# Two decode layers on one core: in the second pass, GpSimd multiplies three of eight key tiles by the query for the first two units

## The chip, the cores and the metric

The kernel runs on one core of a Trainium2 chip. The metric is the device time of one execution in microseconds. TensorE is called PE in the profile, its weight loads PEld, VectorE DVE, ScalarE ACT, GpSimd POOL, and SyncE, which issues nearly all DMAs here, SP.

## The reference

Two rounds of the same two blocks, each with a layer norm ahead and a residual sum behind, for batch 2, one query token, 16 heads of width 256 and 4096 cached keys, all in float32:

```python
q = (x @ wq).reshape(B, Sq, H, Dh).transpose(0, 2, 1, 3)
scores = einsum("bhqd,bhkd->bhqk", q, k_cache) * Dh ** -0.5
o = einsum("bhqk,bhkd->bhqd", softmax(scores), v_cache)
x = x + (o in one row per batch) @ wo
gate, up = x_n @ W_gate, x_n @ W_up
x = x + (relu(gate) * up) @ W_down
```

Attention, feed-forward, attention, feed-forward: both attentions read the whole cache, 32 key rows and 32 value rows of 4 MB each.

## The kernel before

**Units.** One unit `u` is one (head, batch) pair, so an attention pass has 32 units. Its 4096 keys lie as 128 partitions by 32 tiles of 256 numbers. They are handled in four chunks (`c` = 0 to 3) of eight tiles, 1 MB each; values likewise. `order[u]` says which pair a unit is; the second pass begins with the pairs that the first ended with, and most of the keys and values of its first units are still in SBUF.

**Scores.** With one query row a matrix product would leave PE mostly empty, so scores are elementwise products and sums. `score(u, c)` has two ways for a tile. Either DVE does product and sum in one instruction (`scalar_tensor_tensor`, L547), or DVE multiplies several tiles at once (`tensor_mul`, L534) and ACT sums each of these tiles (L540). In the first five units of the second pass (`HASTE`) a chunk is split four and four, except in the first two chunks of unit 0, where DVE does all eight. The query `q_of[u]` of units 0 and 1 lies in PSUM (`po[0]`, `po[1]`); that of unit 2 on is spread to all partitions in SBUF by POOL (`partition_broadcast`, L447).

**Softmax.** `softmax_max(u)`: DVE takes each partition's maximum (L556), POOL the maximum over partitions (`partition_all_reduce`, L558). `softmax_exp(u)`: ACT scales it (L563), takes exponentials and their sum (L567), and POOL adds the sums (L574). `weigh(u, c)` then multiplies a chunk of values by the exponentials on PE (L602).

**What sets the order.** Each engine runs its instructions in the order in which the program wrote them, and waits where it must. SP works off one list of loads in a fixed order (`pump`, L156). A load goes out when the SBUF slot that it is to fill has been released, which `release` does after the last use of what lay there; the loads behind it on the list wait too. Around the change the list reads: the four key chunks of unit 3, into the slots of unit 0's key chunks; the four key chunks of unit 4, into the slots of unit 1's key chunk 0, unit 0's value chunk 0, unit 1's key chunk 1 and unit 0's value chunk 1; two pieces of 2 MB with unit 3's values, after unit 1's key chunk 3 and unit 0's value chunk 3; two pieces of 2 MB with unit 5's keys, after unit 2's key chunk 1 and unit 1's value chunk 1; two of 2 MB with unit 4's values, after unit 2's key chunk 3 and unit 1's value chunk 3; 0.9 MB of weights; then loads of 4 MB and more.

**Start of the second pass.** `first_query` takes the query of unit 0 from the feed-forward block's end, computes the deviation for the layer norm (`Sqrt`, L386) and has ACT do one unread `Exp` (L464), before which ACT loads its table.

Of the kernel before, what the change touches and what calls it, by code (L numbers as in the profile page):

```python
# [14 lines left out]
B, D, H, S, DH, F = 2, 448, 16, 4096, 256, 1792  # L15
P = 128
# [3 lines left out]
CT = 8  # L20
UNIT = CT * DH
NC = NT // CT
# [10 lines left out]

GROUPED = 14
MIDDLE = BLOCKS * PAIR + 1
SUMS = 96
SPACED = 2 * NT + 2
HASTE = 5
# [5 lines left out]
SCALE = DH**-0.5  # L44
# [35 lines left out]
def two_layers(  # L80
# [10 lines left out]
    nc = tc.nc  # L91
# [44 lines left out]
    def pump():  # L136
        while pending:
            (kind, name, c), n = pending[0]
            last = at_of.get((kind, name, c - 1)) if kind in "kv" else None
            if kind == "g":  # L140
                last = MIDDLE - (name + 1) % 2
            at = units.take(n, kind, last)
# [26 lines left out]
    def place(at):  # L169
        packed = max(0, at - BLOCKS * PAIR)  # L170
        return at * UNIT - packed * (UNIT - F)

    def get(*key):
        if key in lies_at:
            return arena[:, lies_at[key] : lies_at[key] + F]
        at = at_of[key]
        return arena[:, place(at) : place(at + 1)]
# [105 lines left out]
    row = consts.tile([P, D], F32, name="row")  # L283
    down = consts.tile([P, D], F32, name="down")
    junk = down[:, :DH]
    spaced = [down[:, DH + i * SPACED : DH + (i + 1) * SPACED] for i in range(2)]
    y_end_row = extra[SUMS : SUMS + B, :TAIL]
    nc.scalar.dma_start(row[:B, :D], x.rearrange("b s d -> (b s) d"))
# [36 lines left out]
    rstd = little("rstd", B, bufs=1)  # L325

    po = [ps_o.tile([P, 2 * DH], F32, name=f"po{i}") for i in range(2)]
# [6 lines left out]
    nc.vector.memset(acc, 0.0)  # L334
    y = acc[SUMS : SUMS + B]

# [46 lines left out]
    def deviation(total):  # L383
        var = ps_s.tile([P, B], F32, name="small")
        nc.tensor.matmul(var, ones.to_broadcast([P, P]), total, start=True, stop=True)
        nc.scalar.activation(rstd, var, AF.Sqrt, bias=eps_t, scale=1.0 / D)  # L386

    def inverse():
        nc.vector.reciprocal(rstd, rstd)

    def attention(order, after, q_first=None, begun=None):
# [3 lines left out]
        nsr = little("nsr", B, bufs=1)  # L395
        sr = little("sr", B, bufs=1)
        aside = []
        q_of, oT_of, s_of, mx_of, p_of, r_of, po_of, pT_of = ({} for _ in range(8))
        n_u = len(order)


        def query_of(u, pq):
            h, b = order[u]
            parts = query_parts(h)
            for c, cols, w in parts:
                nc.tensor.matmul(
                    pq[:, b, cols], xT[:, c, b : b + 1].to_broadcast([P, P]), w,
                    start=(c == 0), stop=(c == parts[-1][0]),
                )
            q_of[u] = pq[:, b, :]  # L410
# [41 lines left out]
        def first_query():  # L452


            if q_first is None:
                total = squares()
                query_of(0, po[0].rearrange("p (b n) -> p b n", b=B))
            else:
                q_of[0] = q_first
                total = begun()  # L460
            deviation(total)
            query_of(1, po[1].rearrange("p (b n) -> p b n", b=B))
            unread = little("sums", 1)
            nc.scalar.activation(unread, eps_t, AF.Exp)  # L464

        def score_block(u, c):

# [39 lines left out]
        def score(u, c):  # L507
            kept = ("k", order[u], c) in after
            if ("k", order[u]) in blocks and not kept and not (ahead and u < HASTE):
                return score_block(u, c)  # L510
            kt = get("k", order[u], c).rearrange("p (t n) -> p t n", t=CT)
            if c == 0:
                s_of[u] = little("scores", NT)
            found = s_of[u][:, c * CT : (c + 1) * CT]
            by_act = 0 if kept else BY_ACT
            part = kt
            if kept and aside:
                by_act = CT // 2 - c % 2
                at = c % 2 * (CT // 2) * DH
                part = aside[0][:, at : at + by_act * DH].rearrange("p (t n) -> p t n", t=by_act)  # L520
            whole = CT
            if ahead and (u < HASTE or u >= n_u - CLOSING):
                by_act = CT // 2 if u > 0 or c > 1 else 0
                last = u == n_u - 1 and c == NC - 1
                whole = by_act if u < HASTE or last else CT
                if whole == CT:
                    by_act = CT // 2 + 1
            whole = whole if by_act else 0
            if kept:
                whole = by_act  # L530
            if by_act:


                nc.vector.tensor_mul(  # L534
                    part[:, :whole, :],
                    kt[:, :whole, :],
                    q_of[u][:, None, :].to_broadcast([P, whole, DH]),
                )
                for t in range(by_act):
                    nc.scalar.activation(  # L540
                        part[:, t, :], part[:, t, :], AF.Copy, accum_out=found[:, t : t + 1]
                    )
            if whole > by_act:
                nc.vector.reduce_sum(found[:, by_act:], kt[:, by_act:, :], axis=AX.X)  # L544
            else:
                for t in range(whole, CT):
                    nc.vector.scalar_tensor_tensor(  # L547
                        junk if kept else kt[:, t, :], kt[:, t, :], 1.0, q_of[u],
                        op0=ALU.mult, op1=ALU.mult, accum_out=found[:, t : t + 1],
                    )  # L550
            if not kept:
                release("k", order[u], c)
# [93 lines left out]
        def project(u):  # L646
# [16 lines left out]
            elif ("h", h, 0) not in after:  # L663
                release("h", h, 0)

        def if_pair(step, u, *more):
            if 0 <= u < n_u:
                step(u, *more)

        first_query()  # L670
        nc.gpsimd.memset(down[:, DH : DH + 2 * SPACED], 0.0)

        ahead = 2 if ("k", order[0], 0) in keep else 0
        for u in range(n_u + 2):

            mixed = ahead and u < HASTE
            if_pair(score, u, 0)
            if_pair(out_add, u - 2)
            if_pair(out_turn, u - 2)
            asked = u % 2 and ahead < u + 1 < n_u  # L680
            if asked and ("h", order[u + 1][0], 0) in after:
                query(u + 1)
                asked = False
            if mixed:
                if_pair(weigh, u - 1, 0)
            if_pair(score, u, 1)
            closing = ahead and u == n_u - 1
            if closing:
                out_keep(u - 2)
                project(u - 2)  # L690
            if mixed:
                if_pair(weigh, u - 1, 1)
            if_pair(score, u, 2)
            if u == 0:
                inverse()
                nc.vector.tensor_scalar_mul(sr, rstd, SCALE)
                nc.vector.tensor_scalar_mul(nsr, rstd, -SCALE)
            if not closing:
                if_pair(out_keep, u - 2)
                if_pair(project, u - 2)  # L700
            if asked:
                query(u + 1)
            if u == n_u - 3 and after:
                slot = units.take(1, "h")
                aside.append(arena[:, place(slot) : place(slot + 1)])
            if ahead and u == 0:
                query(ahead)
            if_pair(softmax_sum, u - 1)
            if mixed:
                if_pair(weigh, u - 1, 2)  # L710
            if_pair(score, u, 3)
            if u % 2 and u < n_u and order[u][0] < GROUPED and order[u][0] % 2:
                release("q", order[u][0] // 2, 0)
            if u == n_u - 1 and aside:
                units.free.add(slot)
                pump()
            if_pair(softmax_max, u)
            if_pair(softmax_exp, u)
            for c in range(NC):
                if not mixed or c == NC - 1:  # L720
                    if_pair(weigh, u - 1, c)
            if_pair(out_copy, u - 1)

    def ffn(last):


        absorb(acc[:SUMS], SUMS, lead, nlead)
        busy(2)
# [53 lines left out]
        pg = proj(banks[0], [(0, 0, True), (1, 1, True), (2, 2, True), (3, 3, False)])  # L782
        add_rows(SUMS, lead, stop=last)
        if last:
            y_left = y[:, : FULL * P]
            left = down[SUMS : SUMS + B, : FULL * P]
            nc.vector.tensor_copy(left, y_left)
# [15 lines left out]
        if last:  # L803
            unit = ident[SUMS : SUMS + B, SUMS : SUMS + B]
            nc.tensor.matmul(y_left, unit, left, start=True, stop=False)
# [211 lines left out]
```

## Time and profile before

| | |
|---|---|
| median of 3 runs | 1314.49 us (1314.07 to 1314.73) |
| the profiled execution | 1314.92 us, of which the span is 1312.7 us |
| busy in the span | DVE 1067.1 us, PE 504.6, POOL 291.8, ACT 193.9 |
| moved by DMA | 561.26 MB, mean 428 GB/s |

The first pass fills the span up to about 650 us, the feed-forward block the stretch to 688 us, and the second pass starts with DVE's first product at 688.45 us. The page's "idle before" of an engine is time in which it waited; "issue" means that the profile shows nothing that it waited for.

### The profile page before, as it was taken

To read this page: it belongs to the slowest core of one execution; us is meant where nothing else is said; L and a number is where in the kernel's file an instruction comes from. 1 tells how busy PE (TensorE), PEld (TensorE's weight loads), DVE (VectorE), ACT (ScalarE), POOL (GpSimd) and SP (SyncE) were. 2 spreads that over 40 slices of the span, in tenths; PEclk is the share of its full clock that TensorE was granted. 3 is DMA by queue.
4 is the path that set the end of the run, shared out by engine and by line. 5 is a ranking of instruction groups with operands and counts; after the bars stand their busy time and mean duration, and the time that the engine had idled before them with its cause. 6 is when DMAs were issued, how large, how long until landed. Compare 5 with 4: busy or idle time off the path is not lost.

```text
span 1312.7 us, 8369 instructions
## 1 busy us (share of the span) xinstructions
PE 504.6 (38%) x3016; PEld 150.8 (11%) x3016; DVE 1067.1 (81%) x709; ACT 193.9 (15%) x784; POOL 291.8 (22%) x168
## 2 busy tenths in 40 slices
PE   3152253332433224424494535322343323433348
PEld 2010011000101001102141101000111000110013
DVE  4988989799897998787619897798999889886892
ACT  1100000010000000122416523000000000012231
POOL 0330412304123050021001253140345004100230
PEclk9566776656776667667697777666776666766669
DMA  9999999999999999999999999999999999999998
GB/s 408 435 434 430 436 432 431 437 424 432 444 419 440 439 430 421 441 423 428 422 400 417 433 425 440 435 439 428 425 439 432 435 429 436 433 434 421 431 421 342
DMA packets 19924, 561.26 MB, mean 428 GB/s; under 512 B 2216, under 2 KB 2348, under 8 KB 6572
## 3 DMA queue, kind: packets, MB, share of 16 engines
q1 hardware_dynamic: 19876, 560.74, 99.5%
q8 instruction: 23, 0.38, 0.1%
q14 instruction: 17, 0.14, 0.0%
q10 hardware_dynamic: 8, 0.00, 0.0%
HBM read 560.73 MB, written 0.00 MB: 427 GB/s over the span
## 4 chain that ended last, share of the span: by engine, by line
DMA 56%; DVE 29%; POOL 7%; PE 4%; issue 2%; ACT 1%; SPq 0%; POOLq 0%; DVEq 0%
DMA arena<-in_vk_dram 50%; DVE tiny L502 15%; DVE arena L488 10%; POOL tiny L574 5%; DMA arena<-in_w_in_dram 3%; DMA arena<-in_w_head_dram 3%; POOL tiny L558 2%; DVE arena L534 2%; DVE arena L547 1%; DMA arena<-in_w_out_dram 1%; PE po L602 1%; PE small L631 1%; ACT arena L540 1%; DVE tiny L544 0%; DVE row L620 0%
## 5 line engine op out<-in xcount | busy, mean ns | idle before, releaser
L488 DVE TENSOR_TENSOR arena<-arena 128x8192 f32<-128x8192 f32 (+2 forms) x53 | 450.9, 8509 | 106.3 <-DMA arena<-in_vk_dram 104.7
L502 DVE TENSOR_REDUCE tiny<-arena 128x32 f32<-128x8192 f32 (+2 forms) x54 | 437.0, 8093 | 0.0
L602 PE MATMUL po<-arena,down 128*4 128x512 f32 x2052 | 314.2, 732 | 186.8 <-ACT down L567 115.5
L558 POOL PARTITION_ALL_REDUCE tiny<-tiny x64 | 95.4, 1490 | 717.1 <-DVE tiny L556 716.3
L631 PE MATMUL small<-tiny,row 128*128 128x2 f32 x128 | 31.2, 348 | 571.9 <-DVE row L620 571.9
L574 POOL PARTITION_ALL_REDUCE tiny<-tiny x64 | 173.8, 2715 | 61.3 <-ACT down L567 61.3
L563 ACT ACTIVATE tiny<-tiny 128x1 f32<-128x1 f32 x64 | 18.8, 294 | 727.8 <-POOL tiny L558 727.8
L602 PEld LDWEIGHTS po<-arena,down 128*4 128x4 f32 x2052 | 65.1, 98 | 406.8 <-issue 226.8
L631 PEld LDWEIGHTS small<-tiny,row 128*128 128x128 f32 x128 | 28.5, 310 | 602.6 <-DVE row L620 602.6
L435 PE MATMUL pq<-arena,xs 128*33 128x512 f32 (+2 forms) x158 | 70.2, 600 | 0.0
L540 ACT ACTIVATE arena<-arena 128x256 f32<-128x256 f32 x134 | 53.9, 403 | 40.8 <-DVE arena L534 40.7
L654 PE MATMUL acc<-arena,tiny 128*2 128x448 f32 x128 | 50.2, 880 | 21.0 <-DVE tiny L644 21.0
L447 POOL PARTITION_BROADCAST arena<-arena x32 | 21.7, 748 | 162.2 <-ACT arena L443 162.2
L494 ACT ACTIVATE arena<-arena 128x256 f32<-128x256 f32 x112 | 44.8, 402 | 79.7 <-DVE arena L488 79.7
L534 DVE TENSOR_TENSOR arena<-arena 128x1024 f32<-128x1024 f32 (+2 forms) x21 | 32.7, 1558 | 4.7 <-PE acc L654 4.7
L443 ACT ACTIVATE arena<-pq 33x512 f32<-33x512 f32 (+1 forms) x16 | 8.8, 548 | 177.2 <-PE pq L435 177.2
L620 DVE SCALAR_TENSOR_TENSOR row<-po,tiny,row 128x256 f32<-128x256 f32 x32 | 15.3, 479 | 22.3 <-ACT row L616 22.3
L644 DVE TENSOR_TENSOR tiny<-small,tiny 128x4 f32<-128x4 f32 x32 | 5.1, 161 | 28.7 <-PE small L631 28.7
L567 ACT ACTIVATE down<-tiny 128x32 f32<-128x32 f32 x64 | 26.6, 416 | 2.2
L435 PEld LDWEIGHTS pq<-arena,xs 128*33 128x33 f32 x158 | 19.2, 131 | 64.4 <-issue 60.0
L540 ACT ACTIVATION_READ_ACCUMULATOR arena<-arena 128x1 f32 x134 | 25.0, 187 | 0.0
L494 ACT ACTIVATION_READ_ACCUMULATOR arena<-arena 128x1 f32 x112 | 20.9, 187 | 0.0
(151 smaller groups left out, 316.8 us busy)
## 6 DMA issues: line engine op xcount, KB each, us to landing
arena<-in_vk_dram SPq DMA_DIRECT2D x17, 4096.0 KB, 41.0
arena<-in_vk_dram SPq DMA_DIRECT2D x16, 2048.0 KB, 34.6
arena<-in_w_pair_dram SPq DMA_DIRECT2D x11, 1792.0 KB, 30.8
arena<-in_vk_dram SPq DMA_DIRECT2D x12, 1024.0 KB, 9.0
arena<-in_w_in_dram SPq DMA_DIRECT2D x12, 896.0 KB, 25.6
arena<-in_vk_dram SPq DMA_DIRECT2D x1, 6784.0 KB
arena<-in_w_head_dram SPq DMA_DIRECT2D x7, 896.0 KB, 31.2
arena<-in_w_out_dram SPq DMA_DIRECT2D x5, 896.0 KB, 19.6
```

Of the source, the lines that this page charges most:

```text
L435: nc.tensor.matmul(q[:, cols], xs[:, c, :], w_c, start=(i == 0), stop=(i == len(parts) - 1))
L488: nc.vector.tensor_mul(part, part, q_of[u][:, None, :].to_broadcast([P, n, DH]))
L494: nc.scalar.activation(kt[:, t, :], kt[:, t, :], AF.Copy, accum_out=s_of[u][:, t : t + 1])
L502: nc.vector.reduce_sum(found, part, axis=AX.X)
L534: nc.vector.tensor_mul(part[:, :whole, :], kt[:, :whole, :], q_of[u][:, None, :].to_broadcast([P, whole, DH]),)
L540: nc.scalar.activation(part[:, t, :], part[:, t, :], AF.Copy, accum_out=found[:, t : t + 1])
L558: nc.gpsimd.partition_all_reduce(mx_of[u], mx, P, RED.max)
L567: nc.scalar.activation(found, s_of.pop(u).rearrange("p (k r) -> p k r", r=2), AF.Exp, bias=nm, scale=sr[:, b : b + 1], accum_out=rs,)
L574: nc.gpsimd.partition_all_reduce(total[:, b : b + 1], rs, P, RED.add)
L602: nc.tensor.matmul(po_of[u][32 * t : 32 * t + 4, (i - 2 * t) * DH : (j - 2 * t) * DH], p_of[u][:, at : at + 4], values[:, i * DH : j * DH] ...
L631: nc.tensor.matmul(pT_of[u][:, c, :], row[:, c * P : (c + 1) * P], pick[:, b : b + B], start=True, stop=True,)
L654: nc.tensor.matmul(acc[at : at + B], oT_of[h][:, c, :], wo[:, c * D : (c + 1) * D], start=(n < 3), stop=(n >= n_u - 3),)
```

## The change

For units 0 and 1 of the second pass, three tiles of each chunk (`POOLED`) are multiplied by the query on POOL, in place in the key slot, and ACT sums these three as before; DVE does the other five in single instructions. Chunk 0 of unit 0 stays with DVE whole. The query is copied for POOL from PSUM into SBUF by DVE, into `row` for unit 0 and `down` for unit 1. POOL's products for chunks 1 to 3 of unit 0 are written at the pass's start, for chunk 0 of unit 1 before DVE's last chunk of unit 0, and for chunks 1 to 3 of unit 1 within that unit. The `Sqrt`, the unread `Exp` with the table load, the memset of `down` and the scales of the exponent come behind `softmax_max(0)`, and the query of unit 2 behind `softmax_exp(0)`. The first pass keeps its order.

```diff
+POOLED = 3
...
         def first_query():
             if q_first is None:
                 total = squares()
                 query_of(0, po[0].rearrange("p (b n) -> p b n", b=B))
+                spread_of(total)
             else:
                 q_of[0] = q_first
                 total = begun()
+                share(0, row[:, :DH], range(1, NC))
+            query_of(1, po[1].rearrange("p (b n) -> p b n", b=B))
+            return total
+
+        def spread_of(total):
             deviation(total)
-            query_of(1, po[1].rearrange("p (b n) -> p b n", b=B))
             unread = little("sums", 1)
             nc.scalar.activation(unread, eps_t, AF.Exp)
+
+        def share(u, room, chunks):
+            if u not in near:
+                nc.vector.tensor_copy(room, q_of[u])
+                near[u] = room
+            for c in chunks:
+                kt = get("k", order[u], c).rearrange("p (t n) -> p t n", t=CT)[:, :POOLED, :]
+                nc.gpsimd.tensor_mul(kt, kt, room[:, None, :].to_broadcast([P, POOLED, DH]))
...
-                by_act = CT // 2 if u > 0 or c > 1 else 0
+                by_act = CT // 2
+                if u < 2:
+                    by_act = POOLED if u + c > 0 else 0
+                    if u == 1 and c < NC - 1:
+                        share(1, near[1], [c + 1])
...
+                if u not in near:
+                    nc.vector.tensor_mul(part[:, :whole, :], ...)
...
             if_pair(score, u, 2)
-            if u == 0:
-                inverse()
-                nc.vector.tensor_scalar_mul(sr, rstd, SCALE)
-                nc.vector.tensor_scalar_mul(nsr, rstd, -SCALE)
+            if u == 0 and ahead:
+                share(1, down[:, :DH], range(1))
...
-            if ahead and u == 0:
-                query(ahead)
...
             if_pair(softmax_max, u)
+            if u == 0 and ahead:
+                nc.gpsimd.memset(down[:, DH : DH + 2 * SPACED], 0.0)
+                spread_of(total)
+                scales()
             if_pair(softmax_exp, u)
+            if ahead and u == 0:
+                query(ahead)
```

POOL at the program's start, the same before and after (line numbers of before). `ident` is the identity matrix that `make_identity` builds; a row "ISA" that names nothing is the one whose instruction the trace calls MODIFY_POOL_CONFIG; "ISA" rows with names are the all-reduces and broadcasts.

```order
masks.py:197 MEMSET ident 128x128
masks.py:199 ISA
masks.py:199 AFFINE_SELECT ident<-ident 128x128
L671 MEMSET down 128x132
L558 ISA
L558 ISA tiny<-tiny 128x1
L574 ISA tiny<-tiny 128x1
L447 ISA arena<-arena 128x256 x2
```

Such a row stands between a tensor instruction such as AFFINE_SELECT and the all-reduces, in either direction; these are the only two in the kernel before. At the start of the second pass, POOL before, from the last unit of the first pass to unit 1:

```order
L558 ISA tiny<-tiny 128x1
L574 ISA tiny<-tiny 128x1
L671 MEMSET down 128x132
L447 ISA arena<-arena 128x256 x2
L558 ISA tiny<-tiny 128x1
L574 ISA tiny<-tiny 128x1
```

The same place after (L481 the products of `share`, L580 and L596 the all-reduces for maximum and sum, L449 the broadcast, L744 the memset):

```order
L481 ISA
L481 TENSOR_TENSOR arena<-arena,row 128x768 x3
L481 TENSOR_TENSOR arena<-arena,down 128x768
L580 ISA
L580 ISA tiny<-tiny 128x1
L744 MEMSET down 128x132
L596 ISA tiny<-tiny 128x1
L449 ISA arena<-arena 128x256 x2
L481 ISA
L481 TENSOR_TENSOR arena<-arena,down 128x768 x3
L580 ISA
L580 ISA tiny<-tiny 128x1
```

Seven products are new, and four of the nameless rows: ahead of unit 0's products, between the fourth product and unit 0's maximum, between the broadcast and unit 1's last three products, and between these and unit 1's maximum.

DVE at the start of the second pass before, units 0 and the first half of unit 1:

```order
L547 SCALAR_TENSOR_TENSOR arena,tiny<-arena,po_101 128x256 x16
L534 TENSOR_TENSOR arena<-arena,po_101 128x1024
L547 SCALAR_TENSOR_TENSOR arena,tiny<-arena,po_101 128x256 x4
L389 RECIPROCAL tiny<-tiny 128x2
L696 TENSOR_SCALAR tiny<-tiny 128x2
L697 TENSOR_SCALAR tiny<-tiny 128x2
L534 TENSOR_TENSOR arena<-arena,po_101 128x1024
L547 SCALAR_TENSOR_TENSOR arena,tiny<-arena,po_101 128x256 x4
L556 TENSOR_REDUCE tiny<-tiny 128x1
L534 TENSOR_TENSOR arena<-arena,po_102 128x1024
L547 SCALAR_TENSOR_TENSOR arena,tiny<-arena,po_102 128x256 x4
```

After, all of units 0 and 1:

```order
L477 COPY row<-po_101 128x256
L569 SCALAR_TENSOR_TENSOR arena,tiny<-arena,po_101 128x256 x18
L477 COPY down<-po_102 128x256
L569 SCALAR_TENSOR_TENSOR arena,tiny<-arena,po_101 128x256 x5
L578 TENSOR_REDUCE tiny<-tiny 128x1
L390 RECIPROCAL tiny<-tiny 128x2
L690 TENSOR_SCALAR tiny<-tiny 128x2
L691 TENSOR_SCALAR tiny<-tiny 128x2
L569 SCALAR_TENSOR_TENSOR arena,tiny<-arena,po_102 128x256 x20
L578 TENSOR_REDUCE tiny<-tiny 128x1
```

The six products of four tiles are gone from DVE, 40 single-tile instructions have become 43, and two copies are added. Unit 1's maximum (the last row) still stands ahead of everything that DVE does for unit 2.

More of the change, by code (lines that the diff above doesn't have):

```diff
@@ L397, in attention @@
         aside = []
+        near = {}
         q_of, oT_of, s_of, mx_of, p_of, r_of, po_of, pT_of = ({} for _ in range(8))
@@ L531, in score @@
             if by_act:
[L534 to L538, printed above, removed]
+                if u not in near:
+                    nc.vector.tensor_mul(
+                        part[:, :whole, :],
+                        kt[:, :whole, :],
+                        q_of[u][:, None, :].to_broadcast([P, whole, DH]),
+                    )
                 for t in range(by_act):
@@ L664, in project, with scales @@
                 release("h", h, 0)
+        def scales():
+            inverse()
+            nc.vector.tensor_scalar_mul(sr, rstd, SCALE)
+            nc.vector.tensor_scalar_mul(nsr, rstd, -SCALE)
         def if_pair(step, u, *more):
@@ L668, in if_pair @@
                 step(u, *more)
-        first_query()
-        nc.gpsimd.memset(down[:, DH : DH + 2 * SPACED], 0.0)
+        total = first_query()
         ahead = 2 if ("k", order[0], 0) in keep else 0
@@ L693, in attention @@
             if_pair(score, u, 2)
-            if u == 0:
-                inverse()
-                nc.vector.tensor_scalar_mul(sr, rstd, SCALE)
-                nc.vector.tensor_scalar_mul(nsr, rstd, -SCALE)
+            if u == 0 and ahead:
+                share(1, down[:, :DH], range(1))
+            if u == 0 and not ahead:
+                nc.gpsimd.memset(down[:, DH : DH + 2 * SPACED], 0.0)
+                scales()
             if not closing:
@@ L717, in attention @@
             if_pair(softmax_max, u)
+            if u == 0 and ahead:
+                nc.gpsimd.memset(down[:, DH : DH + 2 * SPACED], 0.0)
+                spread_of(total)
+                scales()
             if_pair(softmax_exp, u)
+            if ahead and u == 0:
+                query(ahead)
             for c in range(NC):
```

## The prediction

> **What bounds the kernel now.** I read the profile's page first, for what is never idle.
>
> ```profile
> DMA  9999999999999999999999999999999999999998
> q1 hardware_dynamic: 19876, 560.74, 99.5%
> HBM read 560.73 MB, written 0.00 MB: 427 GB/s over the span
> ```
>
> SP's one queue keeps the 16 DMA engines busy for 99.5% of the span. So the kernel is bound by its loads: 1 MB (1.049 million bytes) takes 2.46 us at 427 GB/s, and engine time counts only where a slot comes free so late that the queue runs dry. Next I asked the windows view about the stretch that the change touches (the last number of a row is GB/s).
>
> ```profile
> 690.00:698.00 8.00, 4.08 (x22) 2.91 (x22) 7.97 (x38) 4.80 (x18) 0.70 (x2) 0.97 1.02 422
> 698.00:706.00 8.00, 4.54 (x32) 0.88 (x32) 7.59 (x29) 5.81 (x27) 0.98 (x3) 0.60 1.01 384
> 706.00:714.00 8.00, 1.75 (x16) 0.26 (x12) 7.59 (x29) 5.50 (x26) 1.70 (x2) 0.83 1.00 422
> ```
>
> Here the queue does run nearly dry: 384 GB/s for 8 us instead of 422, so 8 x 38/422 = 0.7 us of transfer is lost. SP's own waits from 690 to 712 us say on whom: on DVE's single-tile scores. SP's loads say how full the queue is: time from issue to landing for the loads issued at 699.7 us (1 MB, after unit 0's key chunk 3), 705.3 (1 MB, after unit 1's chunk 1), 715.9 (2 MB, after unit 2's chunk 1) and 730.4 (0.9 MB), and for one of 0.9 MB at 669.3, in the pause at the feed-forward block.
>
> ```profile
> SPq L156 <- DVE arena L547: 22.5, 8, 4.4
> ...
> L156 SPq DMA_DIRECT2D arena<-in_vk_dram x1: 328/328/328, 699.7 to 699.7; - x1
> DMA to landing us min/median/max: 6.2/6.2/6.2
> ...
> L156 SPq DMA_DIRECT2D arena<-in_vk_dram x1: 328/328/328, 705.3 to 705.3; - x1
> DMA to landing us min/median/max: 9.3/9.3/9.3
> ...
> L156 SPq DMA_DIRECT2D arena<-in_vk_dram x1: 327/327/327, 715.9 to 715.9; - x1
> DMA to landing us min/median/max: 15.8/15.8/15.8
> ...
> L156 SPq DMA_DIRECT2D arena<-in_w_pair_dram x1: 328/328/328, 730.4 to 730.4; - x1
> DMA to landing us min/median/max: 18.2/18.2/18.2
> ...
> L156 SPq DMA_DIRECT2D arena<-in_w_in_dram x1: 328/328/328, 669.3 to 669.3; - x1
> DMA to landing us min/median/max: 5.6/5.6/5.6
> ```
>
> An empty queue thus lands 1 MB about 6.2 us after its issue, so 2 MB after about 8.6 (2.46 more). At 699.7 the queue is empty; afterwards it fills: by 730.4 the wait ahead of a load is 18.2 - 5.6 = 12.6 us. So at this one place a release that comes earlier gains at most 0.7 us, and one that comes later is paid in full once the small store is used up.
>
> **What the change takes from DVE.** The prices are these.
>
> ```profile
> 688.45 0.42 DVE L547 SCALAR_TENSOR_TENSOR arena<-arena,po 128x256 f32<-128x256 f32 x1 [0.66 <-PE po L892]
> 693.92 1.22 DVE L534 TENSOR_TENSOR arena<-arena,po 128x1024 f32<-128x1024 f32 x1
> 679.70 0.56 DVE L819 COPY row<-po 128x384 f32<-128x384 f32 x1 [0.64 <-PE po L813]
> L534 DVE TENSOR_TENSOR arena<-arena,pq 128x768 f32<-128x768 f32 x4 | 3.8, 942 | 0.0
> ```
>
> Sixteen single-tile instructions lie between 688.45 and 693.92: 0.342 us each. Six products of 1.22 go (7.3 us), three singles (1.0) and two copies come; a copy of 256 columns, two thirds of the 0.56 row, is 0.4. Net 4.5 us less for DVE. New DVE times: copy to 688.85; chunk 0 released at 691.6 (the first two releases of before fall due at 688.45 + 8 x 0.342 = 691.2 and 693.9); chunk 1 after five singles at 693.3, chunk 2 at 695.0, copy to 695.4, chunk 3 at 697.1.
>
> **POOL's products.** POOL's rows from the program's start and ahead of the second pass:
>
> ```profile
> 0.73 0.20 POOL masks.py:197 MEMSET ident<- 128x128 f32 x1 [0.29 <-POOLq L1012]
> 12.15 0.28 POOL masks.py:199 TENSOR_SCALAR_AFFINE_SELECT ident<-ident 128x128 f32<-128x128 f32 x1 [11.21 <-issue]
> 39.13 0.38 POOL L558 PARTITION_ALL_REDUCE tiny<-tiny  x1 [26.53 <-DVE tiny L556]
> ...
> 689.50 0.21 POOL L671 MEMSET down<- 128x132 f32 x1 [38.55 <-PE acc L374]
> ```
>
> No row shows a product on POOL. Below, DVE's 0.94 us for the same 128x768; above, I scale POOL's only arithmetic on a tile, 0.28 us for 128x128, by six: 1.7 us. I take 1.7, since it is POOL's own row. Unit 0's three run from 688.9 to 694.0, ahead of DVE's chunk 3, and the first of unit 1 from 695.4, after the second copy, to 697.1. So unit 0 goes well: its last release comes 2.6 us before that at 699.7.
>
> **The nameless rows on POOL.** The order shows four of them in the new stretch. Before has two, both at the program's start, and the trace calls them so:
>
> ```profile
> masks.py:199 POOLq MODIFY_POOL_CONFIG  x2: 11/11/11, 1.0 to 1.0; - x2
> ...
> L558 POOLq MODIFY_POOL_CONFIG  x2: 1/1/1, 12.8 to 12.8; - x2
> ```
>
> MODIFY_POOL_CONFIG itself takes nothing, but the AFFINE_SELECT behind it starts 11.2 us after the memset, its only input, was done, and nothing else is named for that wait. I read it as a switch of POOL's code, of about X = 11.2 us. The second, at 12.8 us, ends somewhere inside 26.3 us of waiting for DVE, so it bounds X only from above; but it shows that a switch hides behind a wait, since the all-reduce then starts at once with its usual 0.38 us. So of the four the first is free: POOL idles for 38.6 us up to 689.5. The other three stand between work that is ready.
>
> The Trainium skill, in GPSIMD Engine Reference, section Instruction dispatch, gives about 6 us, measured 5.95, for the code load behind a MODIFY_POOL_CONFIG. Here the row has nearly twice that. By the Trainium skill the sum below would come to 2 x 5.95 - 5.5 = 6.4 us.
>
> **The chain behind the switches.** Its links from before:
>
> ```profile
> 697.30 0.95 POOL L447 PARTITION_BROADCAST arena<-arena  x2 [7.59 <-ACT arena L443]
> 700.10 0.35 POOL L558 PARTITION_ALL_REDUCE tiny<-tiny  x1 [1.85 <-DVE tiny L556]
> 701.41 0.38 POOL L574 PARTITION_ALL_REDUCE tiny<-tiny  x1 [0.96 <-ACT down L567]
> ...
> 696.78 0.36 ACT L443 ACTIVATE arena<-pq 33x256 f32<-33x256 f32 x1
> ...
> 700.81 0.42 ACT L567 ACTIVATE down<-tiny 128x32 f32<-128x32 f32 x1
> ...
> L540 ACT ACTIVATE arena<-arena 128x256 f32<-128x256 f32 x24 | 9.7, 403 | 5.0 <-DVE arena L534 5.0
> ...
> 721.03 0.19 DVE L556 TENSOR_REDUCE tiny<-tiny 128x1 f32<-128x32 f32 x1 [0.39 <-ACT arena L540]
> ```
>
> - Switch 2: 697.1 to 708.4. Unit 0's maximum, ready on DVE at 697.3, waits for it; before, it started at 700.10. From its start to ACT's end of the exponential are 1.1 us, and 0.1 for handing over: 709.6. PE's `weigh(0)`, and with it value slots, waits for that.
> - ACT then copies the query of unit 2 (0.36) and sums unit 1's chunk 0 (3 x 0.40): released at 711.2. The broadcast ends by 0.52 + 0.95 from the copy's start, at 711.1.
> - Switch 3: 711.1 to 722.3. Products of unit 1's chunks 1 to 3: 724.0, 725.7, 727.4. ACT's three sums: 1.25 us with the handing over, so chunk 1 is released at 725.3 and chunk 3 at 728.7.
> - DVE's maximum of unit 1 stands ahead of its unit 2 and waits for the last of these sums; DVE, done with unit 1's 20 singles at about 697.7 + 6.8 = 704.5, idles for 24 us.
> - Switch 4: 727.4 to 738.6, then unit 1's maximum and exponential. ACT reaches unit 2's sums only at 739.8; eight of them end at 743.0, sixteen at 746.2. Before, DVE took unit 2's maximum at 721.03, so engines run 25 us late.
>
> **The sum, in landings.** After unit 1's chunk 1: issued 725.3, landed 731.5 on an empty queue; before, 705.3 + 9.3 = 714.6. That is 2X - 5.5 = 16.9 us late. The 2 MB after unit 2's chunk 1: issued 743.0, landed 751.6; before, 715.9 + 15.8 = 731.7. That is 3X - 13.7, or 19.9 us late, and the larger of the two counts. Behind it the pieces go out faster than they move, and where engines are 25 us late against the queue's 20, the 12.6 us of store at 730.4 cover the other 5. The lost 0.7 us is inside these landings. What is lost to the queue is lost at the end: 20 us, 1314.9 to 1334.9 us for the profiled execution, 1314.5 to 1334.5 us for the median, which lies 0.4 below it.
>
> The table load costs nothing: ACT's `Sqrt`, load and `Exp` lie beside switch 2, and if that were free they would still end by about 697.2, before the maximum is back. The 4.5 us saved on DVE end in its wait.
>
> **Rivals.**
>
> - *A shorter switch.* Nearly half of the 11.2 us belong to the program's start, where more may be cold, and X is 6. Against it: no row has it shorter. The first landing decides, 2 x 6 - 5.5 = 6.5 us: 1321 us. The figure of the Trainium skill above is this case.
> - *Two kinds of switch.* The 11.2 us were towards tensor instructions, as switch 3; 2 and 4 go to the all-reduces, for which I have only the 26.3 us above. With 6 for those, the first landing gives 6 + 11.2 - 5.5 = 11.7 us: 1326 us.
> - *No switch to pay.* The code stays resident after the first time, or the 11.2 us were the start of the program. Then unit 1's chunks are released at 700.3 to 706.5, chunk 1 at 703.1 (before 705.3), the queue never dries, and the 0.7 us come back: 1313.8 us, not slower. It decides from X below 5.5/2 = 2.75 us. For it: the trace has no packets that I could call code. Against it: the order writes out all four.
> - *A longer switch* under a full DMA queue: 13 us would give 3 x 13 - 13.7 = 25 us, 1340 us.
>
> **How the numbers follow.** X of 11.2 for all three: 0.45, so 1334.5 us. Two kinds: 0.19. Shorter: 0.2. No switch: 0.1. Longer: 0.06. The range takes in all but no switch and the longest: 1319 us (X of 5, 4.5 us) to 1340. A measurement of this kernel can tell about 0.2%, 2.6 us, from no change. Faster by that much needs more than the 0.7 us there are: 0.02. Within it: no switch, or X up to 4: 0.09. Slower: 0.89.
>
> **What would show it.** In the changed kernel's trace: POOL idle for about 11 us by "issue" ahead of unit 0's maximum, of unit 1's second product and of unit 1's maximum; products of about 1.7 us; DVE idle some 24 us ahead of unit 1's maximum, released by ACT; two windows between 705 and 745 us far below 420 GB/s, about 20 us of transfer in sum. Gaps of 6 us give 1321; none, with unit 1's maximum near 705 us, would make the forecast wrong.

## The result, and the profile after

The changed kernel takes 1331.5 us (median of 4 runs, 1330.9 to 1334.5) against 1314.5 us (1314.1 to 1314.7): 1.0134 times, 95% interval 1.0117 to 1.0152, or 17.0 us more. The forecast was 1334.5 us in a range of 1319 to 1340. The profiled execution is the slowest of the four, 1334.5 us; two more traces below show where 3 us of it come from.

From the page of the changed kernel: the loads are the same, and they take longer.

```profile
q1 hardware_dynamic: 19876, 560.74, 98.2%
HBM read 560.73 MB, written 0.00 MB: 421 GB/s over the span
```

The windows view of the changed kernel shows where (last number: GB/s).

```profile
690.00:698.00 8.00, 4.07 (x23) 2.95 (x22) 7.90 (x48) 7.11 (x31) 6.76 (x4) 0.93 1.02 398
698.00:706.00 8.00, 0.00 (x0) 0.00 (x0) 7.30 (x44) 0.07 (x1) 0.12 (x1) 0.50 0.90 371
706.00:714.00 8.00, 2.74 (x16) 0.56 (x20) 0.00 (x0) 2.26 (x10) 1.89 (x5) 0.51 0.08 14
714.00:722.00 8.00, 2.17 (x21) 0.29 (x12) 0.00 (x0) 0.00 (x0) 0.00 (x0) 0.92 0.63 250
722.00:730.00 8.00, 0.00 (x0) 0.00 (x0) 0.83 (x2) 3.92 (x18) 5.32 (x3) 0.50 0.42 148
730.00:738.00 8.00, 0.00 (x0) 0.00 (x0) 6.91 (x27) 0.00 (x0) 0.00 (x0) 0.50 1.03 429
738.00:746.00 8.00, 5.85 (x32) 0.95 (x32) 2.67 (x10) 6.76 (x34) 0.77 (x2) 0.59 0.73 276
```

Against 420 GB/s the windows from 698 us on lose 8 x (49 + 406 + 170 + 272 + 144)/420 = 19.8 us of transfer (the one at 730 loses none); the kernel before lost 0.7 us there. Within a us that is the whole difference of the two profiled executions, 1334.5 - 1314.9 = 19.6 us. From 714 to 722 us DVE, ACT and POOL show no work at all: these three wait for something that shows as no instruction.

POOL's timeline says for whom (start, duration, line; in brackets the idle time before and what ended it; L481 are the products, L580 and L596 the all-reduces for maximum and sum, L449 the broadcast).

```profile
689.72 5.35 POOL L481 TENSOR_TENSOR arena<-arena,row 128x768 f32<-128x768 f32 x3 [38.35 <-DVE row L477]
696.31 1.80 POOL L481 TENSOR_TENSOR arena<-arena,down 128x768 f32<-128x768 f32 x1 [1.24 <-issue]
709.90 0.38 POOL L580 PARTITION_ALL_REDUCE tiny<-tiny  x1 [11.79 <-issue]
...
711.80 0.97 POOL L449 PARTITION_BROADCAST arena<-arena  x2
722.48 5.32 POOL L481 TENSOR_TENSOR arena<-arena,down 128x768 f32<-128x768 f32 x3 [9.71 <-issue]
738.79 0.38 POOL L580 PARTITION_ALL_REDUCE tiny<-tiny  x1 [10.99 <-issue]
```

Three pauses of 11.8, 9.7 and 11.0 us stand between a product and an all-reduce or broadcast, or the other way round, and nothing but "issue" ends them. The first change of kind, ahead of 689.72, is covered by the 38.35 us of waiting for DVE.

Who waits behind them: ACT's scaling of the maximum, which stands ahead of the exponentials (L585), ACT's sums (L562), and DVE's maximum of unit 1 (L578).

```profile
710.31 0.29 ACT L585 ACTIVATE tiny<-tiny 128x1 f32<-128x1 f32 x1 [12.24 <-POOL tiny L580]
724.30 0.42 ACT L562 ACTIVATE arena<-arena 128x256 f32<-128x256 f32 x1 [11.63 <-POOL arena L481]
739.20 0.29 ACT L585 ACTIVATE tiny<-tiny 128x1 f32<-128x1 f32 x1 [10.06 <-POOL tiny L580]
...
729.17 0.19 DVE L578 TENSOR_REDUCE tiny<-tiny 128x1 f32<-128x32 f32 x1 [23.84 <-ACT arena L562]
```

At the end of the chain stands SP. Its waits from 690 to 746 us, and its two loads that the forecast's sum was made of, the 1 MB behind unit 1's chunk 1 and the 2 MB behind unit 2's chunk 1:

```profile
SPq L157 <- ACT arena L562: 35.9, 4, 12.4
...
L157 SPq DMA_DIRECT2D arena<-in_vk_dram x1: 327/327/327, 725.7 to 725.7; - x1
DMA to landing us min/median/max: 4.9/4.9/4.9
...
L157 SPq DMA_DIRECT2D arena<-in_vk_dram x1: 328/328/328, 743.3 to 743.3; - x1
DMA to landing us min/median/max: 7.1/7.1/7.1
```

Landings at 730.6 and 750.4 us, where before had 714.6 and 731.7: 16.0 and 18.7 us late.

### The profile page after: what moved, and what is told of

The parts are those of the page before. It is cut to its first block, busy times and chain, and to the rows that moved or that the text cites. A ratio compares the mean times of both kernels' runs of the same rounds, so it can differ in the third digit from the quotient of the medians.

```text
span 1332.7 us, 8388 instructions
## 1 busy us (share of the span) xinstructions
PE 513.0 (38%) x3016; PEld 153.2 (11%) x3016; DVE 1062.2 (80%) x711; ACT 192.6 (14%) x778; POOL 311.9 (23%) x175
## 4 chain that ended last, share of the span: by engine, by line
DMA 53%; DVE 30%; POOL 8%; PE 4%; issue 3%; ACT 2%; SPq 0%; POOLq 0%; DVEq 0%; ACTq 0%
DMA arena<-in_vk_dram 47%; DVE tiny L519 15%; DVE arena L505 10%; POOL tiny L596 5%; DMA arena<-in_w_in_dram 3%; DMA arena<-in_w_head_dram 3%; POOL tiny L580 2%; DVE arena L569 2%; DVE arena L556 1%; DMA arena<-in_w_out_dram 1%; PE small L653 1%; ACT arena L562 1%; PE pq L437 1%; PE pq L408 0%; DVE row L642 0%
## 5 line engine op out<-in xcount | busy, mean ns | idle before, releaser
L624 PE MATMUL po<-arena,down 128*4 128x512 f32 x2052 | 322.3, 750 | 213.0 <-ACT down L589 139.0
L580 POOL PARTITION_ALL_REDUCE tiny<-tiny x64 | 94.6, 1478 | 723.3 <-DVE tiny L578 700.2
L596 POOL PARTITION_ALL_REDUCE tiny<-tiny x64 | 182.2, 2846 | 61.3 <-ACT down L589 61.3
L585 ACT ACTIVATE tiny<-tiny 128x1 f32<-128x1 f32 x64 | 18.9, 295 | 744.2 <-POOL tiny L580 744.2
L562 ACT ACTIVATE arena<-arena 128x256 f32<-128x256 f32 x131 | 52.7, 404 | 49.0 <-DVE arena L556 35.6
L449 POOL PARTITION_BROADCAST arena<-arena x32 | 21.8, 749 | 144.7 <-ACT arena L445 144.6
L578 DVE TENSOR_REDUCE tiny<-tiny 128x1 f32<-128x32 f32 x64 | 12.0, 187 | 35.5 <-ACT arena L562 32.1
L562 ACT ACTIVATION_READ_ACCUMULATOR arena<-arena 128x1 f32 x131 | 24.5, 187 | 0.0
```

The source lines that it names most:

```text
L562: nc.scalar.activation(part[:, t, :], part[:, t, :], AF.Copy, accum_out=found[:, t : t + 1])
L580: nc.gpsimd.partition_all_reduce(mx_of[u], mx, P, RED.max)
L596: nc.gpsimd.partition_all_reduce(total[:, b : b + 1], rs, P, RED.add)
L624: nc.tensor.matmul(po_of[u][32 * t : 32 * t + 4, (i - 2 * t) * DH : (j - 2 * t) * DH], p_of[u][:, at : at + 4], values[:, i * DH : j * DH] ...
```

## The experiments

Two theories stood against each other: that the uncovered changes of GpSimd between products and all-reduces (called switches here) cost the 17 us, and that GpSimd's slow products, or one of the things that the change moved, cost them. "Before" is the kernel before, run beside each of them on the same chip.

### VectorE's products, everything else as changed

```diff
         def share(u, room, chunks):
-            if u not in near:
-                nc.vector.tensor_copy(room, q_of[u])
-                near[u] = room
+            return
...
-                nc.gpsimd.tensor_mul(kt, kt, room[:, None, :].to_broadcast([P, POOLED, DH]))
...
-                    if u == 1 and c < NC - 1:
-                        share(1, near[1], [c + 1])
```

> The changed kernel, with VectorE doing the products of three tiles itself, so that GpSimd has no product and no change between products and all-reduces; the moved table load, the moved query of unit 2 and the split of the sums between VectorE and ScalarE stay. Theory (the three uncovered switches of GpSimd cost the 17 us): the time of before, 1314.5 us within 1.5. Rival (the move of the table load and of unit 2's query behind unit 0's maximum costs something): several us of the 17 stay, 1317 us or more.

Measured: 1314.7 us, ratio to before 1.0001, interval 0.9992 to 1.0010. The table load, the query of unit 2 and the new split of the sums cost nothing that can be measured. All of the loss belongs to GpSimd's products and what comes with them (the two copies of the query, which are gone here too, among it).

### Only the switches

`dot` is a scratch column; VectorE still multiplies, and nothing is copied.

```diff
             for c in chunks:
-                kt = get("k", order[u], c).rearrange("p (t n) -> p t n", t=CT)[:, :POOLED, :]
-                nc.gpsimd.tensor_mul(kt, kt, room[:, None, :].to_broadcast([P, POOLED, DH]))
+                nc.gpsimd.tensor_mul(dot, dot, dot)
```

> As the kernel with VectorE's products, but GpSimd multiplies one column of a scratch number at the four places where the changed kernel has its products. Nothing waits for these products, and only the alternation between products and all-reduces stays. Theory (switches): the maxima still come late, unit 0's at about 709 and unit 1's at about 734 us, the 2 MB behind unit 2's chunk 1 are issued at about 738.6 and land at about 745.7 instead of 731.7: some 13 us slower than before, 1327 to 1328 us. Rival (the 1.8 us products on GpSimd and the chunks that wait for them are the cost): 1314.5 us within 1.5, since no chunk waits for GpSimd.

Measured: 1320.5 us, 1.0045 times, interval 1.0030 to 1.0060: 6.0 us more. The rival falls, since no chunk waits for GpSimd here, but the theory's 13 us is missed by half. POOL's timeline of this kernel shows the reason.

```profile
658.58 1.00 POOL L477 TENSOR_TENSOR tiny<-tiny 128x1 f32<-128x1 f32 x4 [7.05 <-issue]
700.13 0.38 POOL L576 PARTITION_ALL_REDUCE tiny<-tiny  x1 [40.56 <-DVE tiny L392]
...
712.63 0.86 POOL L477 TENSOR_TENSOR tiny<-tiny 128x1 f32<-128x1 f32 x3 [9.28 <-issue]
724.08 0.38 POOL L576 PARTITION_ALL_REDUCE tiny<-tiny  x1 [10.59 <-issue]
```

The scratch products wait for nothing, so the first four ran already at 658.6 us, and the switch back behind them was covered too: unit 0's maximum is on time at 700.1. Only two switches were uncovered. The experiment did not put the third where it was meant to be; the next one does.

### Three switches, still no chunk waiting

The edit is shown against the kernel with only the switches.

```diff
         def share(u, room, chunks):
+            if u not in copied:
+                nc.vector.tensor_copy(room, q_of[u])
+                copied[u] = room
             for c in chunks:
-                nc.gpsimd.tensor_mul(dot, dot, dot)
+                nc.gpsimd.tensor_mul(dot, dot, copied[u][:, :1])
```

> As the kernel with the switches alone, but GpSimd's one-column products now wait for VectorE's copies of the query, so that they stand where the changed kernel has its products and the switch ahead of unit 0's maximum is uncovered too: three instead of two. Still nothing waits for these products. Theory (each uncovered switch delays the maxima by its length): unit 0's maximum comes at about 706, unit 1's at about 730.5 instead of 724.1, and the 2 MB behind unit 2's chunk 1 land at about 742 instead of 735.8: 1326 us within 1.5. The rest up to 1331.5 us is then the chunks of unit 1 that wait for products behind a switch. Rival (an uncovered switch ahead of unit 0's maximum costs nothing, since unit 1's is what counts): 1320.5 us as with two.

Measured: 1326.0 us, 1.0089 times, interval 1.0074 to 1.0105: 11.4 us more, as the theory had it. POOL's timeline of this kernel, and the row of DVE's timeline with unit 0's maximum on DVE:

```profile
706.06 0.38 POOL L580 PARTITION_ALL_REDUCE tiny<-tiny  x1 [8.33 <-DVE arena L569]
...
719.71 0.78 POOL L481 TENSOR_TENSOR tiny<-tiny,down 128x1 f32<-128x1 f32 x3 [10.78 <-issue]
730.26 0.38 POOL L580 PARTITION_ALL_REDUCE tiny<-tiny  x1 [9.77 <-issue]
...
700.04 0.19 DVE L578 TENSOR_REDUCE tiny<-tiny 128x1 f32<-128x32 f32 x1
```

The maxima stand at 706.1 and 730.3 us (forecast 706 and 730.5). The first pause is put down to DVE, but DVE was done at 700.2 us: the last 5.9 of its 8.3 us are uncovered. This third switch is worth 1326.0 - 1320.5 = 5.5 us. What is left up to 1331.5 us, another 5.5, comes with the real products, but not through chunks that wait for them, as the expectation had it. Compare the trace of a run of the changed kernel that took 1331.2 us (the first of the two further below): unit 0's maximum stands at the same time, 705.96, and unit 1's at 735.21, 5.0 us later than the 730.26 here. Between the two, unit 1's three products take 5.32 us instead of 0.78, and the switch behind them 10.94 instead of 9.77. ScalarE's last sum of unit 1 ends at 725.5 us, long before that, so it is not the chunks that the maximum waits for. The 2 MB behind unit 2's chunk 1 land at 747.0 us there and at 741.9 here. So the products count with their own length, because GpSimd's maximum stands behind them.

### One switch, three products or seven

First with unit 0's products alone:

```diff
-                if u < 2:
+                if u < 1:
                     by_act = POOLED if u + c > 0 else 0
-                    if u == 1 and c < NC - 1:
-                        share(1, near[1], [c + 1])
...
-            if u == 0 and ahead:
-                share(1, down[:, :DH], range(1))
```

> The changed kernel with GpSimd multiplying for unit 0 alone, three products; unit 1 is as before. One uncovered switch is left, ahead of unit 0's maximum. Theory: the switch runs from about 695 to 706.5 us, unit 1's chunk 0 is released at about 710.5 and its MB lands at about 715.4 instead of 709.6: some 6 us slower than before, 1320 us. Rival (cost in proportion to the products, three of seven of the 17 us): 1322 us; rival (only the products of unit 1 are what costs): 1314.5 us.

Measured: 1318.8 us, 1.0033 times, interval 1.0020 to 1.0046: 4.3 us more. That is less than the theory's 1320 and the 1322 us of a cost in proportion, and more than the 1314.5 us of the other rival; the theory's is the nearest. The place is as expected, one pause of 10.8 us ahead of unit 0's maximum; unit 1's chunk 0 was released about 1.4 us earlier than I had it, at 709.05 us.

```profile
689.73 5.37 POOL L481 TENSOR_TENSOR arena<-arena,row 128x768 f32<-128x768 f32 x3 [38.40 <-DVE row L477]
705.86 0.38 POOL L578 PARTITION_ALL_REDUCE tiny<-tiny  x1 [10.77 <-issue]
```

Then all seven ahead of unit 0's maximum:

```diff
-                share(1, down[:, :DH], range(1))
+                share(1, down[:, :DH], range(NC))
...
-                    if u == 1 and c < NC - 1:
-                        share(1, near[1], [c + 1])
```

> The changed kernel with all seven products of GpSimd ahead of unit 0's maximum, so that of the three uncovered switches only one is left. Theory (each uncovered switch is paid): products end at about 703.5, unit 0's maximum comes at about 715, unit 1's chunks 1 to 3 no longer wait for a switch, but ScalarE's sums of unit 1 stand behind unit 0's exponential, so unit 1's chunk 0 is released at about 717.6 and the next MB lands at about 722.5 instead of 709.6: some 12 to 13 us slower than before, 1327 us, and 4 to 5 us faster than the changed kernel. Rival (the products' own time and their reads of the store are the cost, and these are all still there): the changed kernel's 1331.5 us.

Measured: 1322.6 us, 1.0063 times, interval 1.0046 to 1.0080: 8.1 us more than before and 8.9 less than the changed kernel. The rival (the changed kernel's time) falls. The theory's 12 to 13 us is too much because this switch was shorter than any other seen:

```profile
695.42 7.09 POOL L481 TENSOR_TENSOR arena<-arena,down 128x768 f32<-128x768 f32 x4 [1.23 <-issue]
708.31 0.38 POOL L578 PARTITION_ALL_REDUCE tiny<-tiny  x1 [5.80 <-issue]
```

It also shows that the products' own time is not free where a maximum stands behind them: of the 8.2 us by which unit 0's maximum is later than before (708.3 against 700.1), the switch is 5.8.

### Switches that nothing waits for

The kernel before, with a product and an all-reduce on scratch numbers in GpSimd's pause:

```diff
+        if not last:
+            nc.gpsimd.tensor_mul(dots[0], dots[0], dots[0])
+            nc.gpsimd.partition_all_reduce(dots[1], dots[0], P, RED.max)
         absorb(acc[:SUMS], SUMS, lead, nlead)
```

> The kernel before, with a product and an all-reduce of one column each on scratch numbers added to GpSimd, ahead of the feed-forward block's pause, in which GpSimd has nothing else to do for some 38 us. Nothing waits for them; they put two switches into the program, one each way, beside a full stream of loads. Theory (a switch costs only where work stands ready behind it): 1314.5 us within 1.5, and the trace shows each switch as a pause of 10 to 12 us with nothing else named for it. Rival (a switch disturbs the loads or the other engines while it lasts): 1317 us or more, and less than 420 GB/s in those windows.

Measured: 1314.2 us, 0.9996 times, interval 0.9987 to 1.0005. Covered switches cost nothing, and each is seen as a pause, though of 7 us and not of the 10 to 12 expected:

```profile
658.17 0.18 POOL L732 TENSOR_TENSOR tiny<-tiny 128x1 f32<-128x1 f32 x1 [7.22 <-issue]
665.74 0.38 POOL L733 PARTITION_ALL_REDUCE tiny<-tiny  x1 [7.39 <-issue]
```

### The seven products with no switch uncovered

The changed kernel, with what GpSimd would have to switch for moved to other engines. The core of it:

```diff
         def softmax_max(u):
...
+            if u in near:
+                all_of = ps_s.tile([P, P], F32, name="small")
+                nc.tensor.matmul(all_of, mx.to_broadcast([P, P]), ident, start=True, stop=True)
+                nc.vector.reduce_max(mx_of[u], all_of, axis=AX.X)
+                return
             nc.gpsimd.partition_all_reduce(mx_of[u], mx, P, RED.max)
```

> The changed kernel, with the maxima and sums over the partitions of units 0 and 1, and the spreading of the queries of units 2 and 3, done on TensorE, VectorE and ScalarE instead of GpSimd. GpSimd keeps its seven products, and its switch back lies in the wait for unit 2's maximum. Theory (products on GpSimd are harmless where no switch stands in the way): 1313.8 us, 0 to 1 us faster than before, since unit 0's and unit 1's chunks are released some us earlier and the queue's dip of 0.7 us closes. Rival (the products themselves, or VectorE and GpSimd hindering each other, cost part of the 17 us): 1317 us or more.

Measured: 1317.6 us, 1.0024 times, interval 1.0015 to 1.0033. That met the rival's number, not the theory's. Its waits from 697 to 708 us name something else, though: TensorE's 20 products for the next queries (`pq`) stood ahead of ScalarE's sums of unit 1 and of VectorE's copy of a sum.

```profile
ACT arena L430 <- PE pq L409: 3.0, 1, 3.0
DVE tiny L621 <- PE small L620: 2.3, 1, 2.3
```

So these were moved out of the way: the products ahead of unit 0's maximum, the copies behind ScalarE's sums of unit 1, the sums over the partitions to unit 2.

```diff
-            if_pair(sum_up, u - 1)
+            if u == 2 and near:
+                sum_up(0)
+                sum_up(1)
...
                 share(1, down[:, :DH], range(1))
+                query(ahead)
...
             if_pair(score, u, 3)
+            if ahead and u == 1:
+                spread_query(ahead)
...
-            if ahead and u == 0:
-                query(ahead)
```

> The kernel without uncovered switches, mended at the place where its trace shows a new wait: TensorE's 20 products for the queries of units 2 and 3 go ahead of unit 0's maximum, where TensorE idles, ScalarE's copies of them behind its sums of unit 1, and VectorE takes the sums over the partitions of units 0 and 1 only at unit 2. GpSimd's seven products stay. Theory (GpSimd's products are harmless once no switch stands in the way, and the 3 us left were those waits): 1313.5 to 1314.5 us. Rival (the products on GpSimd cost something themselves): 1317 us or more, as before the mending.

Measured: 1314.4 us (median of 11, one of which took 1320.4), 1.0003 times, interval 0.9994 to 1.0011, with all seven products on POOL:

```profile
688.74 5.37 POOL L493 TENSOR_TENSOR arena<-arena,row 128x768 f32<-128x768 f32 x3 [37.77 <-DVE row L489]
695.33 1.80 POOL L493 TENSOR_TENSOR arena<-arena,down 128x768 f32<-128x768 f32 x1 [1.22 <-PE pq L409]
697.07 0.21 POOL L777 MEMSET down<- 128x132 f32 x1
697.24 5.33 POOL L493 TENSOR_TENSOR arena<-arena,down 128x768 f32<-128x768 f32 x3
720.69 1.23 POOL L597 PARTITION_ALL_REDUCE tiny<-tiny  x1 [18.12 <-DVE tiny L590]
```

The switch back lies in the 18 us of waiting for unit 2's maximum. So GpSimd's seven products cost nothing here, where neither a switch nor an all-reduce of units 0 and 1 stands behind them, and they are no gain either. The queue's dip was not closed but spread: 406, 399 and 415 GB/s in the three windows from 690 us where before had 422, 384 and 422. None of these kernels beats the kernel before.

### How long a switch lasts

A look at lengths: a second pair in GpSimd's pause, and a pair behind the sums of units 8 and 12 of both passes.

```diff
             nc.gpsimd.partition_all_reduce(total[:, b : b + 1], rs, P, RED.add)
+            if u in (8, 12):
+                nc.gpsimd.tensor_mul(dots[0], dots[0], dots[0])
+                nc.gpsimd.partition_all_reduce(dots[1], dots[0], P, RED.max)
```

> The kernel before with pairs of a one-column product and a one-column all-reduce on scratch numbers, put where GpSimd has nothing else to do: two pairs in the feed-forward block's pause, and one pair each behind the sums of units 8 and 12 of both passes. It is a look at how long a switch lasts beside different loads. If a switch has one length, and those of 9.3 to 11.8 us in the second pass hold something else too, all are near 7.3 us; if the length follows the loads beside it, the four in the pause (rows of 7 KB) are near 7.3 us and those beside the large loads of units 8 and 12 are longer, 10 us and more.

Measured, in one run: 1318.2 us; some of the pairs held up the next maximum. POOL's rows of the pause, and of unit 8 in the first and unit 12 in the second pass:

```profile
659.62 0.18 POOL L736 TENSOR_TENSOR tiny<-tiny 128x1 f32<-128x1 f32 x1 [7.25 <-issue]
667.47 0.38 POOL L737 PARTITION_ALL_REDUCE tiny<-tiny  x1 [7.67 <-issue]
676.09 0.18 POOL L736 TENSOR_TENSOR tiny<-tiny 128x1 f32<-128x1 f32 x1 [8.24 <-issue]
686.76 0.38 POOL L737 PARTITION_ALL_REDUCE tiny<-tiny  x1 [10.49 <-issue]
...
211.38 0.18 POOL L580 TENSOR_TENSOR tiny<-tiny 128x1 f32<-128x1 f32 x1 [11.29 <-issue]
220.13 0.38 POOL L581 PARTITION_ALL_REDUCE tiny<-tiny  x1 [8.57 <-issue]
...
924.49 0.18 POOL L580 TENSOR_TENSOR tiny<-tiny 128x1 f32<-128x1 f32 x1 [11.88 <-issue]
934.02 7.91 POOL L581 PARTITION_ALL_REDUCE tiny<-tiny  x1 [9.35 <-issue]
```

Neither expectation holds: there is no one length, and the four in the pause are not alike; the other four of units 8 and 12 lasted 8.7 to 10.6 us. What sets it stays open.

### The changed kernel twice more

> The changed kernel once more, for a second trace of its three uncovered switches, since the profiled run of it (1334.5 us, switches of 11.8, 9.7 and 11.0 us, 32.5 in sum) was 3 us over the median. If the switches' length differs from run to run and sets the time, a run of 1331.5 us has a sum of some 29.5 us, and each us of the sum is one us of time. If the sum is again 32.5 us in a run that is 3 us shorter, the difference lies elsewhere.

> As the run before it: the changed kernel a third time. Sum of the three uncovered switches against the time of the same run, one us for one us if the switches set it.

One run each, 1331.2 and 1332.0 us. POOL's three rows of the first, then of the second:

```profile
705.96 0.38 POOL L580 PARTITION_ALL_REDUCE tiny<-tiny  x1 [8.74 <-issue]
...
718.95 5.32 POOL L481 TENSOR_TENSOR arena<-arena,down 128x768 f32<-128x768 f32 x3 [10.12 <-issue]
735.21 0.38 POOL L580 PARTITION_ALL_REDUCE tiny<-tiny  x1 [10.94 <-issue]
```

```profile
706.84 0.38 POOL L580 PARTITION_ALL_REDUCE tiny<-tiny  x1 [8.69 <-issue]
...
719.77 5.33 POOL L481 TENSOR_TENSOR arena<-arena,down 128x768 f32<-128x768 f32 x3 [10.06 <-issue]
736.22 0.38 POOL L580 PARTITION_ALL_REDUCE tiny<-tiny  x1 [11.12 <-issue]
```

The sums are 29.8 and 29.9 us against 32.5 in the first trace: 2.7 and 2.6 us less, and the times are 3.3 and 2.6 us less. The first switch alone, 11.8 us in one run and 8.7 in two, is 3.1 us of the difference. Three runs fit the rule of one us for one us; they do not show it finely, since the first of the two also began its products 0.9 us earlier (688.83 against 689.72 us).

## Why the prediction was right

Point by point, along its own steps.

- **The bound.** Right: only the stretch where SP's queue runs dry counts, and the transfer lost in the windows (19.8 us, of which 0.7 were lost before too) is within a us the loss of the profiled execution (19.6 us). It lies in four windows, not in the two forecast.
- **DVE and unit 0.** Right: chunk releases, seen as SP's loads at 692.5, 694.2, 695.9 and 698.0 us, come 0.9 us behind the forecast; 0.7 of that is a later start of the second pass in this run. The 4.5 us saved on DVE ended, as said, in its wait of 23.8 us (forecast 24).
- **The products.** 1.80 us each instead of 1.7: the scaled row was 6% short.
- **The switches.** The case with three of 11.2 us was the likeliest, and the sum of 33.6 compares with 32.5, 29.8 and 29.9 us measured. That they are paid where work stands ready, and free behind a wait, is shown by the kernels above: none uncovered 1314.4 (with the products) and 1314.2 us (without), two 1320.5, three 1326.0, three with the real products 1331.5 us. The number of switches is no price list, though: with one uncovered it was 1318.8 or 1322.6 us, by what stood around it. That the pause is a switch of GpSimd's code, as the prediction reads it, no trace shows; what the traces show is that it stands behind a MODIFY_POOL_CONFIG at each change of kind. That one length holds for all was wrong: the row from the program's start is near the upper end of 5.8 to 11.9 us. *A shorter switch* and *a longer switch* as forecast are out. *Two kinds of switch* is out too: the changed kernel's one towards the products is the middle or the shortest of its three (9.7 to 10.1 us), and in the kernel before with hidden ones they are 7.2 and 7.4. *No switch to pay* is out, since the changes of kind go on to bring their pauses late in the program too (at 934 us in the run on lengths). With no all-reduce left between the products the time is 1314.4 us, not the 1313.8 of that case.
- **The Trainium skill's figure.** GPSIMD Engine Reference, section Instruction dispatch, puts the code load behind a MODIFY_POOL_CONFIG at some 6 us. Of the pauses here one is that short (5.8 us); the three that set the time are 8.7 to 11.8. With 5.95 us the prediction's sum gives an estimate of 1321 us, 10 us short.
- **The sum.** 2X - 5.5 and 3X - 13.7 with the lengths of the profiled run: the second gives 32.5 - 13.7 = 18.8 us, and the 2 MB landed 18.7 us late. Two errors are in it and nearly cancel. The landing on an empty queue was mis-sized: 6.2 and 8.6 us were forecast, 4.9 and 7.1 measured. The row for 6.2 was no empty queue; the MB ahead of that load was still moving. Against it, the switches apart, the load went out 1.4 us later than the sum has it; 0.7 of that is the later start, the rest some tenths of the copies, the products and the handing over. So the near hit on this landing is in part luck. Behind it the queue does not run dry again (420 GB/s and more from 746 to 802 us), as forecast.
- **The median.** The forecast's 1334.5 us is 3.0 over it. The mis-sized term is X: in the two further traces, whose times lie at the median, the three switches are 3.8 and 3.7 us shorter than 3 x 11.2.
- **The table load** behind the maximum costs nothing: shown by the kernel with VectorE's products, 1.0001 times before.

## What to carry to other kernels

An engine that changes between two kinds of work can pay for the change far more than for the work: here 7 products of 1.8 us brought three pauses of about 10 us, and VectorE, ScalarE and the loads stood behind them. Look in the trace for idle time that only "issue" ends, and at what kinds stand on both sides; then group the work by kind, or put the change into a wait that is there anyway, where it costs nothing. And before moving work off an engine, ask whether its time is the bound at all: with every switch hidden the change gained nothing.

## What the hardware showed that was not expected

- A pause between a product and an all-reduce lasted 5.8 to 11.9 us, in both directions, and was not the same at one place from run to run (11.8, 8.7 and 8.7 us ahead of unit 0's maximum). How full the DMA queue is does not explain the length: 11.0 us lay beside 429 GB/s (the window from 730 us), and the 7.2 and 7.4 us of the hidden switches beside 413 and 420 GB/s.
- A memset brings no such pause on either side: it follows the all-reduce at once in the changed kernel, and in the last version above it stands between two products, which start at 695.33 and 697.24 us, with no idle time.
- The DMA queue landed 1 MB 4.9 us and 2 MB 7.1 us after the issue, once it had run empty or all but empty; in the two further traces it was 4.5 us for the 1 MB, and 7.3 and 7.2 us for the 2 MB.
